# State attention and a hard-swish feed-forward on one NeuronCore: the second softmax's exponentials moved through DRAM, and heads paired four apart

## The chip, the cores and the metric

The kernel runs on one core of a Trainium2 chip. The metric is the device time of one execution in microseconds (us), median of several runs. The program's five engines run side by side, each in the order of its own queue: TensorE (PE; its weight loads are shown as PEld), VectorE (DVE), ScalarE (ACT), GpSimd (POOL) and SyncE (SP), which here issues nearly all DMAs.

## The reference

Two parts. An attention between tokens and a small state, for 8 batches and 8 heads, with 512 tokens, 32 states and 64 features a head:

```python
scores = scale * x @ state^T;   a  = softmax(scores)     # over 32 states
xread  = a @ state
scores2 = scale * state @ x^T;  a2 = softmax(scores2)    # over 512 tokens
sread  = a2 @ x
y = concatenate([xread, sread], tokens)                  # 544 rows a batch, 8 x 64 features
```

and a feed-forward over the 8 x 544 rows: `h = y @ w_in` (512 to 2048), `g = h * clip(h + 3, 0, 6) / 6`, `out = g @ w_out` (2048 to 512). `x` and `state` come as float32, the two weights as float64.

## The kernel before

**Tiling and stages.** The hidden width of 2048 is taken in two sweeps of 1024. In each sweep the 8 batches' 512 tokens are units of eight steps (one step is 128 hidden columns); between the sweeps stand two units for the 8 x 32 state rows. `xread @ w_in` is never made by way of `xread`: the kernel multiplies `state` into `w_in` first (`wprime`, W'), and then the weights `a` with W'. Products run in three passes of float32 parts (`hi*hi + hi*lo + lo*hi`), with ACT making each `hi` and DVE each `lo` (`split`). In the second sweep seven half-size products stand for eight (`seconds`, line 1164).

**The attention of batch b** (1 to 7) runs beside the first sweep of batch b-1. `load_turned` (line 611) brings `x[b]` in blocks of 32 x 32 by DMA and DVE turns the blocks (line 725). `scores_by_columns` (859) multiplies it with the state on PE. `tokens_by_columns` makes `a`, `states` (899) the exponentials of the second softmax, with 128 rows that are states of four heads, two such groups. For `sread` the exponentials must be turned so that tokens lie on partitions: DVE turns their 32 x 32 blocks (line 971), and `weights_moved` (951) then puts the blocks in place by 16 DMAs from SBUF to SBUF a batch (line 979), each 32 partitions and 256 pieces of 128 bytes. `tokens_read` (988) multiplies them with `x` on PE (line 1007); for b > 0 it rides in the same PE entry as the next batch's scores, so that entry waits for the moves and for the next batch's turned `x` alike.

**Pairing.** A partition row of 128 features is a pair of heads (2q, 2q+1), for q = 0 to 3, in `w_in`, `x` and `state` alike. `load_turned` therefore takes 16 transfers a batch, one for each head and half of its features: 64 KB, 512 pieces of 128 bytes. `w_in` comes in 13 transfers (`weight`, line 484), each over all 128 partitions.

**The order.** All work is entered in a `Plan` (line 141) with an engine, a cost, what it reads and writes and, for DMAs, a size and a number of pieces. `Plan.order` is a list scheduler at build time: of what could start within 0.3 us it takes the entry with the least rank, and the ranks are the 2701 numbers in `RANKS` (line 24). The result is a fixed order for each of the five queues. A DMA stands in SP's queue with its wait: what is behind it is not issued before it. `first_of[n]` is the PE entry of step n; up to the first of them, at 19.4 us, filler transposes (line 1642) are put on PE where the plan has a gap; no filler comes after.

Of the kernel before, what the change touches and what calls it, by code (L numbers as in the profile page):

```python
# [10 lines left out]
F32 = mybir.dt.float32  # L11
# [273 lines left out]
def tile_state_attention_then_hardswish_ffn(  # L285
# [38 lines left out]
    kept = ctx.enter_context(tc.tile_pool(name="kept", bufs=1, space=bass.MemoryType.DRAM))  # L324

    x_v = x.rearrange("b h (j p) d -> b j p h d", p=P)
    st_v = state.rearrange("b (q u) n d -> b q n u d", u=NG)

    ident = cpool.tile([P, P], F32, name="ident")
    make_identity(nc, ident)  # L330
# [1342 lines left out]
```

## Time and profile before

| | |
|---|---|
| median of 3 runs | 647.98 us (646.3 to 648.6) |
| the profiled execution | 644.92 us, of which 642.6 us are the span from the first to the last instruction |
| PE busy | 632.0 us, 98% of the span; 4386 matmuls |
| DVE, ACT, POOL busy | 520.6, 346.1, 18.3 us |
| granted TensorE clock | 1.00 throughout |
| DMA | 82.52 MB in 162326 packets, 129760 of them under 512 bytes |

PE counts as busy from the start of a matmul to its modelled end, and matmuls overlap: one of 512 columns lasts 0.39 us, but the next begins 0.23 us after it. So the loss on PE is read from the start of one to the start of the next, not from the busy share. Issuing a DMA is not counted as busy time of SP; how long an issue took is read from the timeline, the chain of waits and the view of a line.

### The profile page before, as it was taken

Reading aid. Unit: us, or ns where it says so; the run is one execution under the profiler, and the core shown is the slowest. Engines: PE = TensorE matmul, PEld = TensorE weight load, DVE = VectorE, ACT = ScalarE, POOL = GpSimd, SP = SyncE. Lnnn points to the kernel's source line nnn. Section 1 sums busy time; section 2 is a strip of 40 time slices with the busy share of each in tenths; the row PEclk is TensorE's granted clock in tenths of the full one; section 3 lists DMA queues with packets and bytes.
Section 4 is the critical chain, followed back from the end, with each engine's and each line's share of the span. In section 5 each row is a group of like instructions: output and inputs, shape, how many; then the busy total and the mean of one; then the engine's idle time right before and its main releaser. Section 6 shows DMA issues by size and latency. Waiting matters only on the chain.

```text
span 642.6 us, 11571 instructions
## 1 busy us (share of the span) xinstructions
PE 632.0 (98%) x4386; PEld 525.5 (82%) x4386; DVE 520.6 (81%) x946; ACT 346.1 (54%) x611; POOL 18.3 (3%) x22
## 2 busy tenths in 40 slices
PE   8999999999999999999999999999999999999997
PEld 6466867877677768778898887999999999999996
DVE  5998788988878859787388837999999888979873
ACT  5866444555456543545365747666464655464441
POOL 0000000000000000000000000000001000001100
PEclk9999999999999999999999999999999999999999
DMA  8986695957749648343303876153524442522433
GB/s 301 267 194 145 163 174 100 239 96 194 149 85 249 165 114 158 91 75 94 70 14 119 275 253 210 50 132 67 132 34 99 99 91 33 116 58 34 65 67 66
DMA packets 162326, 82.52 MB, mean 128 GB/s; under 512 B 129760, under 2 KB 147040, under 8 KB 162144
## 3 DMA queue, kind: packets, MB, share of 16 engines
q1 hardware_dynamic: 158304, 73.80, 44.9%
q0 software_dynamic: 3824, 7.87, 8.4%
q8 instruction: 34, 0.56, 0.4%
q14 instruction: 20, 0.16, 0.1%
q10 hardware_dynamic: 144, 0.13, 0.1%
HBM read 47.17 MB, written 30.93 MB: 122 GB/s over the span
## 4 chain that ended last, share of the span: by engine, by line
PE 80%; DMA 6%; DVE 6%; SPq 5%; ACT 2%; issue 2%; DVEq 0%; ACTq 0%
PE ps_h L1052 27%; PE acc L1164 23%; PE acc L1052 23%; DMA raw<-in_x_dram 2%; SPq L979 2%; SPq L622 2%; PE ps_s L635 1%; DMA raw<-in_moe_w_out_dram 1%; PE acc L1337 1%; PE ps_s L1473 1%; DMA early<-in_moe_w_in_dram 1%; DMA raw<-in_moe_w_in_dram 1%; PE acc L1473 1%; DVE g L1308 1%; PE ps_h L1007 1%
## 5 line engine op out<-in xcount | busy, mean ns | idle before, releaser
L1052 PE MATMUL acc<-w_out_hi,g_hi 128*128 128x512 f32 x296 | 118.5, 400 | 0.1
L1052 PE MATMUL acc<-w_out_hi,g_lo 128*128 128x512 f32 x296 | 115.5, 390 | 0.6 <-DVE g_lo L408 0.6
L1052 PE MATMUL acc<-w_out_lo,g_hi 128*128 128x512 f32 x296 | 115.5, 390 | 0.0
L1164 PE MATMUL acc<-w_out_hi,tmp 128*128 128x256 f32 x360 | 88.9, 283 | 0.0
L1052 PE MATMUL ps_h<-aT_hi,wp_hi 128*128 128x512 f32 (+1 forms) x228 | 84.1, 369 | 1.6 <-DVE wp_lo L408 0.8
L1305 ACT ACTIVATE g<-ps_h,three 128x512 f32<-128x512 f32 (+1 forms) x80 | 51.2, 647 | 62.1 <-PE ps_h L1052 54.9
L1052 PE MATMUL ps_h<-aT_lo,wp_hi 128*128 128x512 f32 (+1 forms) x228 | 82.4, 361 | 0.0
L1052 PE MATMUL ps_h<-aT_hi,wp_lo 128*128 128x512 f32 (+1 forms) x228 | 82.1, 360 | 0.0
L1289 ACT ACTIVATE G<-ps_h,three 128x512 f32<-128x512 f32 x64 | 43.9, 690 | 55.0 <-PE ps_h L1052 45.8
L1052 PEld LDWEIGHTS acc<-w_out_hi,g_hi 128*128 128x128 f32 x296 | 55.6, 188 | 19.4 <-issue 6.1
L1308 DVE SCALAR_TENSOR_TENSOR g<-g,ps_h 128x512 f32<-128x512 f32 (+1 forms) x80 | 49.8, 629 | 26.2 <-ACT g L1305 25.9
L1164 PE MATMUL acc<-w_out_hi,g_lo 128*128 128x256 f32 x240 | 67.9, 283 | 0.0
L1164 PE MATMUL acc<-w_out_lo,g_hi 128*128 128x256 f32 x240 | 67.9, 283 | 0.0
L1164 PE MATMUL acc<-w_out_hi,g_hi 128*128 128x256 f32 x240 | 67.8, 282 | 0.0
L1164 PEld LDWEIGHTS acc<-w_out_hi,tmp 128*128 128x128 f32 x360 | 66.7, 192 | 0.3
L1052 PEld LDWEIGHTS acc<-w_out_hi,g_lo 128*128 128x128 f32 x296 | 55.6, 188 | 13.5 <-DVE g_lo L408 1.4
L1052 PEld LDWEIGHTS acc<-w_out_lo,g_hi 128*128 128x128 f32 x296 | 55.6, 188 | 10.7 <-issue 0.3
L407 ACT CAST g_hi<-g 128x512 fp32r<-128x512 f32 (+1 forms) x74 | 42.3, 585 | 36.2 <-DVE g L1308 18.7
L408 DVE TENSOR_TENSOR g_lo<-g,g_hi 128x512 fp32r<-128x512 f32 (+1 forms) x74 | 46.3, 639 | 11.5 <-ACT g_hi L407 8.2
L1291 DVE SCALAR_TENSOR_TENSOR G<-G,ps_h 128x512 f32<-128x512 f32 x64 | 43.4, 683 | 12.6 <-ACT G L1289 12.1
L407 ACT CAST g_hi<-G 128x512 fp32r<-128x512 f32 (+1 forms) x64 | 38.0, 605 | 28.6 <-PE acc L1164 20.1
L1052 PEld LDWEIGHTS ps_h<-aT_hi,wp_hi 128*128 128x128 f32 x228 | 43.1, 189 | 11.8 <-DVE G L1291 1.7
(167 smaller groups left out, 1236.6 us busy)
## 6 DMA issues: line engine op xcount, KB each, us to landing
out_dram<-ot SPq DMA_DIRECT2D x8, 1024.0 KB, 4.6
W<-G SPq DMA_DIRECT2D x16, 512.0 KB, 4.0
out_dram<-ot POOLq DMA_DIRECT2D x15, 512.0 KB, 5.7
raw<-in_x_dram SPq DMA_DIRECT2D x112, 64.0 KB, 3.3
xb<-in_x_dram SPq DMA_DIRECT2D x28, 256.0 KB, 4.3
raw<-in_moe_w_out_dram SPq DMA_DIRECT2D x11, 511.8 KB, 5.8
wp_lo<-W SPq DMA_DIRECT2D x40, 128.0 KB, 3.0
raw<-in_moe_w_in_dram SPq DMA_DIRECT2D x8, 511.0 KB, 4.4
```

The costliest lines, as they stand in the source:

```text
L407: first = S_(cost, rank, lambda: nc.scalar.copy(hi(), src()), reads, [writes[0]], after)
L408: V(cost, rank, lambda: nc.vector.tensor_tensor(lo(), src(), hi().bitcast(F32), op=ALU.subtract), [*reads, writes[0]], [writes[1]])
L622: nc.sync.dma_start(t[rows, i].rearrange("t (a c) -> t a c", c=NS), x[b, 4 * g + 2 * i + u, :, k * NS : (k + 1) * NS].rearrange("(a t) c - ...
L635: nc.tensor.matmul(out[u][cols, :], made["stT", b][rows, cols], moving(q)[rows], start=True, stop=True,)
L979: nc.sync.dma_start(dst[:, :, q], src[:, :, c])
L1052: nc.tensor.matmul(ps, l, r, start=start and k == 0, stop=stop and k == n - 1)
L1164: nc.tensor.matmul(out, left(a, l), right(b, r), start=p == 0 and z == 0 and y == 0, stop=p == FPS // 2 - 1 and y == 2, skip_group_check=True)
L1289: S_(0.68, n - 1.5, lambda: nc.scalar.activation(g(), by_pass(), AF.Relu, bias=three, scale=-1.0 if turned_sign(FPS + i) else 1.0), [ps], ...
L1291: V(0.63, n - 1.5, lambda: nc.vector.scalar_tensor_tensor(g(), g(), 6.0, by_pass(), op0=ALU.min, op1=ALU.mult), [ps], [g_key])
L1305: in_turn["g", n] = S_(cost + 0.05, rank, lambda: nc.scalar.activation(g(), bank(ps)[:, :width], AF.Relu, bias=three, scale=-1.0 if turned ...
L1308: V(cost, rank, lambda: nc.vector.scalar_tensor_tensor(g(), g(), 6.0, bank(ps)[:, :width], op0=ALU.min, op1=ALU.mult), [ps], [g_key])
L1473: nc.tensor.matmul(bank(banks[q // 2][u])[:, q % 2 * W : (q % 2 + 1) * W], st[l]()[rows, q], wp(r)[rows, q], start=y == 0, stop=y == 2, sk ...
```

## The change

Nothing is added to or taken from PE's, DVE's or ACT's work; the transfers, the pairing of heads and the ranks change.

- `weights_moved`: four transfers write the turned blocks of a batch to a DRAM tile (`there`, 32 x 32 x 128 floats; each 32 partitions, 1024 pieces of 128 bytes), and one (`back`) reads the 512 KB tile into SBUF in place, 1024 pieces of 512 bytes. `back` waits for the four. It was 16 transfers within SBUF.
- Heads are paired four apart: (q, q+4). The two heads of one slot in `load_turned` are then neighbours, so one transfer brings two: 8 a batch of 128 KB and 1024 pieces, for 16. `state`'s views, batch 0's `x` and the index in `tokens_read` follow the pairing.
- A row of `w_in` on the partitions is then no even stride, so each of its 13 loads becomes two of 64 partitions (`load(u)`).
- The plan's cost of `wprime` is entered lower (0.18 + 0.85 a chunk for 0.26 + 0.95), which touches the order alone.
- `RANKS` is new: 2581 numbers. The 120 entries less are 56 for `x`, 77 for the moves, and 13 more for `w_in`. The order of all queues may differ from before.

```diff
@@ RANKS: 2701 numbers before, 2581 after @@
...
@@ -324,7 +319,7 @@
     kept = ctx.enter_context(tc.tile_pool(name="kept", bufs=1, space=bass.MemoryType.DRAM))
 
     x_v = x.rearrange("b h (j p) d -> b j p h d", p=P)
-    st_v = state.rearrange("b (q u) n d -> b q n u d", u=NG)
+    st_v = state.rearrange("b (u q) n d -> b q n u d", u=NG)
 
     ident = cpool.tile([P, P], F32, name="ident")
     make_identity(nc, ident)
@@ -340,7 +335,7 @@
     nc.gpsimd.memset(apart, 0.0)
 
 
-    w_in_v = w_in.bitcast(U16).rearrange("(q p) e -> p q e", p=P)
+    w_in_v = w_in.bitcast(U16).rearrange("(u q d) e -> u d q e", u=NG, q=NQ)
     w_out_v = w_out.bitcast(U16).rearrange("(f p) e -> p f e", p=P)
 
     BANKS = {f"acc{j}": 1 for j in range(J)} | {"ps_h": 2, "ps_s": 2}
@@ -473,15 +468,16 @@
             t = t.rearrange("p i e -> p (i e)").rearrange("p (q f) -> p q f", q=NQ)
             return t if i is None else t[:, :, i * P : (i + 1) * P]
 
-        def load():
+        def load(u=0):
             t = pieces().bitcast(U16)
             flat = t.rearrange("p i e k -> p i (e k)")
             if kind == "in":
                 flat = flat.rearrange("p i e -> p (i e)").rearrange("p (q e) -> p q e", q=NQ)
-                src = w_in_v[:, :, 4 * k * P + 1 : 4 * (k + n) * P]
-            else:
-                src = w_out_v[:, k : k + n, 1:]
-            nc.sync.dma_start(flat[:, :, : flat.shape[2] - 1], src)
+            flat = flat[:, :, : flat.shape[2] - 1]
+            if kind == "out":
+                nc.sync.dma_start(flat, w_out_v[:, k : k + n, 1:])
+                return
+            nc.sync.dma_start(flat[u * D : (u + 1) * D], w_in_v[u, :, :, 4 * k * P + 1 : 4 * (k + n) * P])
 
         def top_of(i):
             t = tops[:, plan.home["top", (kind, k + i)]]
@@ -503,14 +499,17 @@
                 d, low, 13, top_of(i).bitcast(U32), op0=ALU.logical_shift_right, op1=ALU.bitwise_or
             )
 
-        Q(load_rank, 524.288 * n, load, writes=[key], pieces=128 * n if kind == "out" else 512,
-          late=2.0 if k >= FPS else 0.5)
+        late = 2.0 if k >= FPS else 0.5
+        keys = [(*key, "u", u) for u in range(NG)] if kind == "in" else [key]
+        for u in range(len(keys)):
+            Q(load_rank, 524.288 * n / len(keys), lambda u=u: load(u), writes=[keys[u]],
+              pieces=128 * n if kind == "out" else 256, late=late)
         lo = key + ("lo",)
         wide = 0.08 + 0.54 * n
         for i in range(n):
             top = ("top", (kind, k + i))
-            S_(0.62, rank, lambda i=i: upper(i), [key], [top])
-            V(0.62, rank, lambda i=i: join(i), [key, top],
+            S_(0.62, rank, lambda i=i: upper(i), keys, [top])
+            V(0.62, rank, lambda i=i: join(i), [*keys, top],
               w_in_keys(k + i, k + i + 1) if kind == "in" else [(*lo, i)])
         if kind == "in":
             return
@@ -602,8 +601,8 @@
         load_state(0, rank)
         for q in range(NQ):
             hs = slice(q * NG, (q + 1) * NG)
-            def load(hs=hs):
-                nc.sync.dma_start(raw()[:, hs], x[0, hs].rearrange("h (p j) d -> p h j d", j=J))
+            def load(hs=hs, q=q):
+                nc.sync.dma_start(raw()[:, hs], x[0, q::NQ].rearrange("h (p j) d -> p h j d", j=J))
             Q(rank + 0.1 * q, 262.144, load, writes=[(*raw_key, q)], pieces=256, late=0.5)
             V(0.37, rank, lambda hs=hs: nc.vector.tensor_copy(x_tile(0)[:, hs], raw()[:, hs]),
               [(*raw_key, q)], [(*key, "q", q)])
@@ -613,19 +612,16 @@
 
         for g in range(NG):
             key = ("raw", ("x", b, g))
-            for i in range(2):
-                for u in range(2):
-                    for k in range(D // NS):
-                        def load(g=g, i=i, u=u, k=k, key=key):
-                            t = get(key, lambda: stage.tile([P, 2, S], F32, name="raw"))
-                            rows = slice((u * D // NS + k) * NS, (u * D // NS + k + 1) * NS)
-                            nc.sync.dma_start(
-                                t[rows, i].rearrange("t (a c) -> t a c", c=NS),
-                                x[b, 4 * g + 2 * i + u, :, k * NS : (k + 1) * NS].rearrange(
-                                    "(a t) c -> t a c", t=NS
-                                ),
-                            )
-                        Q(rank, 140.0, load, writes=[(*key, i, u, k)], after=after, pieces=512, cost=0.54)
+            for u in range(NG):
+                for k in range(D // NS):
+                    def load(g=g, u=u, k=k, key=key):
+                        t = get(key, lambda: stage.tile([P, 2, S], F32, name="raw"))
+                        rows = slice((u * D // NS + k) * NS, (u * D // NS + k + 1) * NS)
+                        heads = slice(NQ * u + 2 * g, NQ * u + 2 * g + 2)
+                        nc.sync.dma_start(
+                            t[rows].rearrange("t i (a c) -> t (i a) c", c=NS),
+                            x[b, heads, :, k * NS : (k + 1) * NS].rearrange("h (a t) c -> t (h a) c", t=NS))
+                    Q(rank, 280.0, load, writes=[(*key, u, k)], after=after, pieces=1024, cost=0.54)
 
     def all_heads(b, out, moving):
 
@@ -672,7 +668,7 @@
             for c, _, _, n, fs, bs in work:
                 all_heads(b, [bank(key)[:, :n] for key in bs], lambda q: w_in_of(units[k][0] * CPS + c)[:, q, fs])
 
-        at = T(0.26 + sum(0.95 * w[3] / CH for w in work), rank, run,
+        at = T(0.18 + sum(0.85 * w[3] / CH for w in work), rank, run,
                [("stT", b)] + [key for c, f0, f1, *_ in work for key in w_in_keys(
                    units[k][0] * FPS + c * FPC + f0, units[k][0] * FPS + c * FPC + f1)],
                [key for w in work for key in w[5]], after)
@@ -711,7 +707,7 @@
                     for k in range(NG):
                         nc.tensor.matmul(
                             out[..., k], made["st_raw", b][:, k],
-                            ident.rearrange("p (q u m) -> p q u m", q=NQ, u=NG)[:, :, u], start=True, stop=True)
+                            ident.rearrange("p (u q m) -> p q u m", q=NQ, u=NG)[:, :, u], start=True, stop=True)
             turned_first[0] = T(0.65, rank, turn_first, [("st_raw", b)], [st], after)
 
         def put_state():
@@ -724,7 +720,7 @@
                 key = ("raw", ("x", b, q // 2))
                 V(0.7, rank, lambda q=q, key=key: nc.vector.transpose(
                     xT(b, q), made[key][:, q % 2]),
-                    [(*key, q % 2, u, k) for u in range(2) for k in range(D // NS)], [xT_key(b, q)], after)
+                    [(*key, u, k) for u in range(2) for k in range(D // NS)], [xT_key(b, q)], after)
                 continue
             ps = (banks[q] if banks else "ps_s", ("T", b, q))
 
@@ -971,13 +967,19 @@
             V(0.62, rank, lambda g=g: nc.vector.transpose(
                 made_of(blocks_key)[:, g], tmp(("tmp", ("e2", b, g)))),
                 [("tmp", ("e2", b, g))], [(*blocks_key, g)])
-        for c in range(P // NS):
-            for q in range(NQ):
-                def move(c=c, q=q):
-                    src = made_of(blocks_key)[quarter(q)].rearrange("p g (j c n) -> p (g j) c n", j=J, n=NS)
-                    dst = made_of(e2T_key(b, 0))[quarter(c)].rearrange("p g (j q n) -> p (g j) q n", j=J, n=NS)
-                    nc.sync.dma_start(dst[:, :, q], src[:, :, c])
-                Q(rank, 60.0, move, [(*blocks_key, g) for g in range(NG)], [e2T_key(b, 0, c, q)], pieces=256, cost=0.66, late=0.5)
+        there = lambda: get(("kept", (b, "e2")), lambda: kept.tile([NG * S // NS, NS, P], F32, name=f"e{b}"))
+        for q in range(NQ):
+            def move(q=q):
+                nc.sync.dma_start(
+                    there()[:, :, quarter(q)].rearrange("m r n -> r m n"),
+                    made_of(blocks_key)[quarter(q)].rearrange("p g (m n) -> p (g m) n", n=NS))
+            Q(rank, 140.0, move, [(*blocks_key, g) for g in range(NG)], [("kept", (b, "e2"), q)], pieces=1024, cost=0.6)
+
+        def back():
+            nc.sync.dma_start(
+                made_of(e2T_key(b, 0)).rearrange("p g (j m) -> p (g j) m", m=P),
+                there().rearrange("(y c) r m -> (c r) y m", c=P // NS))
+        Q(rank, 524.0, back, [("kept", (b, "e2"), q) for q in range(NQ)], [e2T_key(b, 0)], pieces=1024, cost=0.5)
 
     def put(c, ps, cols):
         V(0.28, URGENT, lambda: nc.vector.tensor_copy(
@@ -991,8 +993,7 @@
         x_parts = [(*read_key(b), "q", q) for q in range(NQ)] if b == 0 else [
             (*read_key(b), j) for j in range(J)]
         t_key = ([e2T_key(b, g) for g in range(NG)] if b == 0 else
-                 [e2T_key(b, g, c, q) for g in range(NG if b < TURNED else 1)
-                  for c in range(P // NS) for q in range(NQ)])
+                 [e2T_key(b, 0)])
         pr, sr_key = (tag, ("D", b)), ("tmp", ("sr", b))
         by_group = lambda t: t[:, : NG * D].rearrange("p (u d) -> p u d", u=NG)
 
@@ -1007,7 +1008,7 @@
                         nc.tensor.matmul(
                             bank(pr)[cols, u * D : (u + 1) * D],
                             e2T(b, u)[:, j * P + q * NS : j * P + (q + 1) * NS],
-                            x_tile(b, True)[:, NG * q + u, j, :],
+                            x_tile(b, True)[:, NQ * u + q if b else NG * q + u, j, :],
                             start=(j == 0),
                             stop=(j == J - 1),
                         )
```

## Rows read from the trace of the kernel before

**Rows 1.** The page's first part: engine, busy us, share of the span, instructions.
```profile
PE 632.0 (98%) x4386; PEld 525.5 (82%) x4386; DVE 520.6 (81%) x946; ACT 346.1 (54%) x611; POOL 18.3 (3%) x22
```

**Rows 2.** Stretches: us, busy us (instructions) by engine, granted clock, DMA share, GB/s.
```profile
20.00:240.00 220.00, 216.39 (x1461) 158.10 (x1467) 184.98 (x335) 124.50 (x218) 0.00 (x0) 1.00 0.71 164
...
400.00:639.00 239.00, 239.00 (x1640) 222.32 (x1638) 205.35 (x378) 124.93 (x223) 17.41 (x15) 1.00 0.38 77
639.00:642.60 3.60, 0.06 (x1) 0.00 (x0) 0.76 (x2) 0.00 (x0) 0.00 (x0) 1.00 0.22 73
```

**Rows 3.** What PE waited for: us in total, times, longest us.
```profile
PE ps_s L712 <- DMA st_raw<-in_state_dram: 1.1, 1, 1.1
PE ps_h L1052 <- DVE wp_lo L408: 0.8, 1, 0.8
...
PE ps_h L1007 <- DMA raw<-raw: 0.8, 2, 0.6
PE acc L1052 <- DVE g_lo L408: 0.6, 1, 0.6
...
PE ps_h L1052 <- DVE ot L408: 0.3, 1, 0.3
PE ps_h L1052 <- DVE g L1308: 0.2, 1, 0.2
```

**Rows 4.** Timeline of PE: start us, us, instruction, [idle before, its releaser].
```profile
106.53 0.39 PE L1052 MATMUL ps_h<-aT_lo,wp_hi 128*128 128x512 f32 x1
106.76 0.39 PE L1052 MATMUL ps_h<-aT_hi,wp_lo 128*128 128x512 f32 x1
107.35 0.50 PE L1052 MATMUL ps_h<-aT_hi,wp_hi 128*128 128x512 f32 x1 [0.20 <-DVE g L1308]
...
110.73 0.40 PE L1007 MATMUL ps_h<-xb,raw 128*32 128x64 f32 x4 [0.59 <-DMA raw<-raw]
```

**Rows 5.** The chain that ended last, 95 to 165 us: start us, us, what.
```profile
100.93 0.61 SPq L979
...
109.28 1.96 DMA raw<-raw
...
155.64 3.25 SPq L622
...
160.00 2.47 DMA raw<-in_x_dram
...
163.89 1.20 PE acc L1052 x4
```

**Rows 6.** Lines that issue DMAs: issue ns min/median/max, first and last start us.
```profile
L622 SPq DMA_DIRECT2D raw<-in_x_dram x112: 311/488/3255, 22.0 to 250.7; - x112
...
L979 SPq DMA_DIRECT2D raw<-raw x112: 585/609/1397, 68.4 to 307.4; - x112
...
L593 SPq DMA_DIRECT2D xb<-in_x_dram x28: 384/488/5663, 60.8 to 280.6; - x28
...
L484 SPq DMA_DIRECT2D early<-in_moe_w_in_dram x5: 384/469/796, 3.2 to 23.2; - x5
```

**Rows 7.** DMA issues: count, KB each, median us from issue to landing.
```profile
raw<-in_x_dram SPq DMA_DIRECT2D x112, 64.0 KB, 3.3
...
a<-tmp SPq DMA_DIRECT2D x14, 256.0 KB, 2.7
...
aT_lo<-a SPq DMA_DIRECT2D x7, 512.0 KB, 4.4
```

**Rows 8.** The page's third part: a DMA queue's packets, MB, share of 16 engines.
```profile
q1 hardware_dynamic: 158304, 73.80, 44.9%
```

**Rows 9.** The chain's pieces on DVE in the start.
```profile
11.85 0.63 DVE raw L502
...
15.96 0.60 DVE w_in L502
```

**Rows 10.** Timeline of PE: the first product of a step.
```profile
19.40 3.68 PE L1269 MATMUL ps_h<-w_in,tmp 128*128 128x512 f32 x8
```

221 rows, old and new, of the table RANKS are left out of this document.

## The prediction

> **What bounds the kernel now.** I read the busy shares first: PE 98%, DVE 81% [rows 1]. The stretches then show that PE's share is no mean over unlike stages: from 400 us to the last product PE is busy the whole time, and after 639 us only the last stores are left, 3.6 us [rows 2]. Between 20 and 240 us, the first sweep, PE is busy 216.4 of 220 us, DVE 185.0, and the DMA engines 0.71 of the time [rows 2]. So the change, whose instructions run from 22 to 307 us [rows 6], can win only what PE loses in the first sweep or before it. It doesn't touch PE's own work: the same 4386 matmuls [rows 1].
>
> How much PE loses there is in the list of its waits. Leaving out the start, five entries stand in the first sweep: 0.8 (W' part late from DVE), 0.8 (the moved exponentials, two times), 0.6, 0.3 and 0.2 us, together 2.7 us [rows 3]. A wait costs more than its idle time. Matmuls of 512 columns start 0.23 us apart (106.53, 106.76); over the 0.20 us wait the step is 0.59, so 0.36 is lost, 0.16 more than the wait [rows 4]. Six waits by 0.16 make about 1.0, so the whole loss is some 3.7 us: 1.1 at the moved exponentials, 2.6 at the four others.
>
> Then the chain of waits says what stands behind these. Before the product at 110.7 stand the sixteen issues of line 979 one after another, 0.61 us each with 0.04 between, and then the landing of the last, 1.96 us [rows 4, 5]. Before the late `g_lo` that PE waits for until 163.89 stand issues of line 622, one of which took 3.25 us, and a landing of 2.47 us of `x` for which DVE stood still [rows 5]. Both lead to SP's queue. That is where the change takes work away.
>
> **The change part by part.** *SP's issues.* Removed are 56 transfers of `x` at 0.49 + 0.04 us, 29.7 us, and 112 moves at 0.61 + 0.04, 72.8 us [rows 5, 6]. Added are 28 writes, which the trace doesn't show in this form: between 0.49 (line 593, as many pieces) and 3.26 us (the longest of line 622, when the queue was full) [rows 6]; I take 0.65, that of line 979, the same tile read in pieces of the same size: 18.2 us. Seven reads back at 0.46, the early weight loads' least 0.38 to their median 0.47 [rows 6]: 3.2 us. Thirteen more loads of `w_in` at 0.47 + 0.04: 6.6 us. Net, SP has 74.5 us less to issue in 285 us. A transfer of `x` of 1024 pieces is not dearer to issue than one of 512: line 593 has 1024 and the same median, 488 ns [rows 6]. [...]
>
> *Time from the first move to usable data.* Before: 15 issues at 0.65 and a landing of 1.96, 11.7 us [rows 5]. After: the last of four writes is issued at 1.95 and lands 2.7 later, as the stores of `a` do [rows 7], at 4.6 us; `back` lands 4.4 later, as the 512 KB reads of `a` do [rows 7]: 9.0 us. From above, still without any penalty for DRAM: the queue took 512 pieces of `x` every 0.53 us [rows 6], so 4096 pieces take up to 4.2 us, with 2.0 for the landing and 4.4 for the read 10.6 us. So the exponentials come 1.1 to 2.7 us earlier, and the two waits for them, 1.1 us with their restarts, go. Next late at that PE entry is the next batch's turned `x`, which the same queue brings and which comes earlier too. I take the whole 1.1; bounds 1.1 and minus 1.1, if other reads come to wait.
>
> *A wait is added.* `back` waits in SP's queue for four writes, 2.7 to some 4.3 us after the last issue. Behind it stand transfers of `x` and the weights, for which DVE (line 725) and ACT wait. Against it stand the 7.2 us a batch that SP saves at the moves (16 x 0.65 less 4 x 0.65 less 0.46, and 0.1 for gaps). So what is behind is issued earlier by 2.9 us or more even if nothing useful stands between.
>
> *The four other waits*, 2.6 us, are DVE results that are late. One of them leads to `x` transfers by the chain [rows 5]; for the others DVE's load of 185 in 220 us [rows 2] is as good a reason. I count half, 1.3 us; bounds 2.6, and minus 2.6 where the new order makes as many of its own.
>
> *`w_in` in halves.* Before the first product at 19.40 us [rows 10] three of its loads become six: 3 x 0.51 = 1.5 us more on SP, in front of the loads of `w_out`. The path to the first product runs through batch 0's softmax on DVE, which `w_out`'s late arrival doesn't hold, so I count nothing. If that cover is gone it costs up to 1.5 us. On the other side two joins of weight digits stand among the softmax steps, 0.63 and 0.60 us [rows 9]; if the new ranks put them behind, the start is up to 1.2 us shorter. Batch 0's `x` has as many transfers and pieces as before, and the pairing of its heads costs nothing.
>
> *Bytes.* The reads back are new traffic: 7168 packets of 512 bytes. The mean packet of SP's queue took 0.449 x 642.6 x 16 / 158304 = 29 ns of one engine [rows 8], so 13 us of all sixteen in 285 us, 0.05 on a share of 0.71 [rows 2]. That alone stays hidden.
>
> *The pieces' size.* In this trace pieces of 128 bytes only come out of DRAM (`x`) or stay in SBUF (the moves); none goes into DRAM. [...]
>
> The sum: 1.1 + 1.3 = 2.4 us. On the profiled execution, 644.92 us (642.6 and 2.3 around the span), that gives 642.5. The median of the runs shown is 3.06 us above that execution, so 645.6 us.
>
> **The rivals.**
> *More is won.* All 3.7 us of waits go and the two joins leave the start: 4.9 us, 643.1. For it: the chain leads to SP in both places looked at. Against it: DVE stays at 84% in that stretch.
> *Nothing is won.* The late DVE results are late because DVE is full, the two waits for the exponentials turn into waits for `x`, and the new order has stalls like the old: 648.0, give or take 2. [...]
> *Slower: small writes into DRAM.* If a piece of 128 bytes into DRAM takes twice the time of one of `x`, the four writes take 8.4 us, and the way is 8.4 + 2.0 + 4.4 = 14.8 us, 3.1 later than before. Seven reads wait for it, and PE's order is fixed, so the loss is up to 21.7 us; of the seven only two waited before, so the others had some slack, and I take half, 10.9 us: 658.9. It decides from the point where the 4096 pieces take over 11.7 - 2.0 - 4.4 = 5.3 us, 1.3 times what `x` takes. While `back` stands, `x` of the next batch also stands behind it. [...]
>
> **How the numbers follow.** Forecast 0.48, its own range 643.4 to 647.4 (a gain of 0.6 to 4.6 us: the 1.1 with none or all of the 2.6, and 0.9 for the start either way); more 0.17; nothing 0.17; slower 0.18. For the slower case 1.3 times is not far, but a write to DRAM of 2 KB pieces lands in 2.7 us without a sign of trouble, and what is late there is first covered by slack. About 0.5%, 3.2 us, is what a measurement of this kernel can tell from no change: below 644.7 or above 651.2. Faster by more: 0.16 of the second case and 0.20 of the first, 0.36. Slower by more: 0.15 of the last and 0.01 of the third, 0.16. Within: 0.48. The range, 642.0 to 650.5, leaves out some 0.04 below (all bounds together, start included) and 0.15 above.
>
> **What would show it.** In the profile after: SP's issues of `x` halved in number with a median near 0.5 us; the writes near 0.65 us each; from the first write to the landing of `back` 9 to 10.6 us (over 11.7: the slower case); no PE wait for `raw` at the read of tokens; PE's waits in the first sweep near 1.3 us in place of 2.7; the first product within a us of 19.4; from 400 us on nothing changed but the offset. The prediction is wrong if PE waits at several of the seven reads, if DVE's waits for `x` grow behind a standing `back`, or if the start moves by over 1.5 us.

## The result, and the profile after

The changed kernel takes 653.71 us (median of 4, 653.13 to 654.62), the kernel before 648.19 us beside it (4 runs, 646.3 to 648.6): a ratio of 1.0092, 95% interval 1.0069 to 1.0115. It is slower by 0.9%, above the range of the forecast. The profiled execution took 654.62 us, its span 652.8 us. Against the profiled execution of before, 644.92 us, that is 9.7 us, more than the 5.5 between the medians: that one lies at the fast end of its runs.

PE's work is the same but for 16 more filler transposes. The profile page's first part, and the stretches (us, busy us and instructions by engine, granted clock, DMA share, GB/s):

```profile
PE 635.9 (97%) x4402; PEld 529.4 (81%) x4402; DVE 521.9 (80%) x946; ACT 343.4 (53%) x611; POOL 18.3 (3%) x22
```

```profile
20.00:240.00 220.00, 211.84 (x1481) 155.05 (x1482) 186.33 (x338) 120.44 (x213) 0.00 (x0) 0.98 0.91 183
400.00:639.00 239.00, 238.86 (x1657) 222.31 (x1657) 210.32 (x387) 129.15 (x233) 16.42 (x15) 1.00 0.39 83
```

Against [rows 1, 2]: from 400 us to the last product nothing is different but the offset. In the first sweep the DMA engines are busy 0.91 of the time, not 0.71, for 183 GB/s against 164: 28% more time for 12% more bytes. (The share adds up the times of all packets over 16 engines, so it can pass 1.)

What PE waited for (us in total, times, longest us):

```profile
PE ps_s L631 <- DVE w_in L498: 3.0, 1, 3.0
PE ps_h L1053 <- DVE g L1309: 2.2, 1, 2.2
...
PE ps_h L1008 <- DMA raw<-e: 1.0, 1, 1.0
PE acc L730 <- DVE xb L607: 0.9, 2, 0.6
PE ps_h L1053 <- DVE aT_lo L403: 0.7, 1, 0.7
PE acc L1053 <- DVE g_lo L403: 0.6, 1, 0.6
```

The two longest are new against [rows 3], and both lie in the first 45 us, by PE's timeline:

```profile
22.39 3.60 PE L1270 MATMUL ps_h<-w_in,tmp 128*128 128x512 f32 x8
29.01 0.67 PE L631 MATMUL ps_s<-w_in,stT 64*32 64x256 f32 x16 [3.02 <-DVE w_in L498]
...
43.98 0.77 PE L1053 MATMUL ps_h<-aT_hi,wp_hi 128*128 128x512 f32 x1 [2.24 <-DVE g L1309]
44.55 0.63 PE L1053 MATMUL ps_h<-aT_lo,wp_hi 128*128 128x512 f32 x1
44.98 0.63 PE L1053 MATMUL ps_h<-aT_hi,wp_lo 128*128 128x512 f32 x1
...
47.70 0.39 PE L1053 MATMUL ps_h<-aT_hi,wp_hi 128*128 128x512 f32 x1
47.92 0.39 PE L1053 MATMUL ps_h<-aT_lo,wp_hi 128*128 128x512 f32 x1
```

The first product comes at 22.39 us, not 19.40 [rows 10]. Behind the second wait the matmuls start 0.43 us apart (44.55, 44.98), not 0.22 (47.70, 47.92). The stretches behind both waits show a mean granted clock of 0.57 and 0.52 of full: by the trace's records the clock was 0.50 for 3.4 us from 30.3 us, 1.3 us behind the end of the 3.02 us wait, and for 3.4 us from 44.0, where the 2.24 us wait ended. At half pace that is some 3 us more, an estimate from these two times:

```profile
30.00:34.00 4.00, 4.00 (x6) 1.36 (x7) 2.79 (x6) 3.59 (x8) 0.00 (x0) 0.57 1.02 172
...
44.00:47.50 3.50, 3.50 (x9) 2.78 (x10) 3.50 (x6) 2.75 (x4) 0.00 (x0) 0.52 1.04 315
```

One thing about this column has to be known. The view shows 1.00 also where the trace has no record of the clock, and the records begin only at 4.7 us before and at 6.4 us after. Until then PE ran at its lower pace in both: matmuls of 128 columns started 213 ns apart, behind it 109. So the "1.00 throughout" of the kernel before holds from 4.7 us on.

I laid the two executions over each other by the PE work still to be done, worked out from all matmuls at their steps; what a step is priced at moves these figures by up to 1 us. The changed kernel is 3.0 us behind at its first product, some 11 at 42 us of the time before, then 9.8 at 274 and 8.6 to 8.8 from 438 us to the last product. So all of this loss, and more, arises in the first 45 us, ahead of the first of the moves through DRAM (75.1 us); behind that the change wins some 2 us. The spans differ by 10.2 us: another 1.4 come behind the last product, where the last store of 128 KB landed in 3.2 us and not in 1.8.

The chain of waits up to 50 us says through what (start us, us, what):

```profile
3.24 5.46 DMA early<-in_moe_w_in_dram
...
8.72 13.33 DMA early<-in_moe_w_in_dram
...
33.51 7.51 DMA early<-in_moe_w_in_dram
...
41.12 0.77 ACT tops L493
...
41.92 1.32 DVE w_in L498 x2
43.24 0.61 DVE g L1309
```

Half a load of `w_in`, 511 KB, took 13.33 us to land. The wait for `g` at 43.98 is one for `w_in` too: DVE stood for it and made `g` late. The page's list of DMA issues (KB each, median us to landing) has for the early loads, first before, then after:

```profile
early<-in_moe_w_in_dram SPq DMA_DIRECT2D x3, 1023.0 KB, 8.8
```

```profile
early<-in_moe_w_in_dram SPq DMA_DIRECT2D x6, 511.5 KB, 10.8
```

Half the bytes take longer, though these times hold the wait behind earlier transfers too. The stretches of the start, before and then after, show that it isn't only a queue that stands:

```profile
10.00:15.00 5.00, 5.00 (x62) 3.60 (x59) 4.89 (x10) 4.73 (x10) 0.00 (x0) 1.00 1.04 397
15.00:20.00 5.00, 4.52 (x55) 3.16 (x43) 4.93 (x11) 3.36 (x9) 0.00 (x0) 1.00 1.08 345
20.00:30.00 10.00, 9.24 (x36) 3.33 (x34) 9.23 (x20) 9.25 (x19) 0.00 (x0) 1.00 1.05 282
```

```profile
10.00:15.00 5.00, 4.44 (x64) 3.83 (x63) 3.33 (x6) 3.62 (x9) 0.00 (x0) 1.00 1.04 331
15.00:20.00 5.00, 4.62 (x42) 2.79 (x40) 4.79 (x12) 2.69 (x5) 0.00 (x0) 1.00 1.07 198
20.00:30.00 10.00, 6.79 (x47) 4.04 (x48) 6.13 (x14) 4.98 (x12) 0.00 (x0) 1.00 1.07 240
```

The DMA engines are full in both; between 15 and 20 us, at shares of 1.08 and 1.07, they move 345 GB/s before and 198 after. Worked out from the trace's packets between 15 and 20 us, one of 2046 bytes, which is a piece of a row of `w_in`, takes 97 ns before and 180 after. The early loads are 3 x 1023 + 2 x 511 KB, 4.2 MB; at 345 GB/s they take 12.1 us of full engines, at 198 GB/s 21.2, 9.0 us more. This estimate is most of the 11 by which the kernel is behind at 42 us; the lower clock after the waits adds to it.

### The profile page after: what moved, and what is told of

It reads as the page before. It is cut to its first block, busy times and chain, and to the rows that moved or that the text cites. A ratio compares the mean times of both kernels' runs of the same rounds, so it can differ in the third digit from the quotient of the medians.

```text
span 652.8 us, 11434 instructions
## 1 busy us (share of the span) xinstructions
PE 635.9 (97%) x4402; PEld 529.4 (81%) x4402; DVE 521.9 (80%) x946; ACT 343.4 (53%) x611; POOL 18.3 (3%) x22
## 4 chain that ended last, share of the span: by engine, by line
PE 82%; DMA 9%; DVE 5%; ACT 1%; SPq 1%; issue 1%; DVEq 0%; ACTq 0%
PE ps_h L1053 27%; PE acc L1053 25%; PE acc L1165 23%; DMA early<-in_moe_w_in_dram 4%; DMA raw<-in_moe_w_in_dram 3%; PE ps_s L631 2%; DMA early<-in_moe_w_out_dram 1%; PE ps_s L1474 1%; PE ps_h L1008 1%; PE acc L1474 1%; DMA raw<-e 1%; ACT tops L493 1%; PE ps_h L631 1%; DVE g L1309 1%; DVE tmp L721 1%
```

## The experiments

Theory: a transfer into one half of the partitions moves its bytes at about half the rate, and nothing else of the change loses time. Rivals: the extra issues; some other part of the change (order, pairing, moves); that the halves read rows of DRAM lying close together.

**The halves alone, in the kernel before.**

```diff
-            nc.sync.dma_start(flat[:, :, : flat.shape[2] - 1], src)
...
+            for u in range(2):
+                nc.sync.dma_start(flat[u * D : (u + 1) * D], src[u * D : (u + 1) * D])
```

> The kernel before with one edit: each of the 13 loads of w_in is issued as two transfers of 64 partitions, as in the changed kernel, in the same place of SP's queue; pairing, moves and ranks are those of before. Theory A (a transfer into 64 partitions moves its bytes at little more than half the rate): packets of 2046 bytes take about 180 ns in place of 97, PE waits for weights in the first 60 us, and the time goes up by 6 to 11 us, to 654 to 659. Theory B (the new ranks made the loss, the halves cost only 13 more issues of about 0.5 us): at most 1.5 us more, 648 to 650. Theory C (the clock drop after idle stretches is the first cause): no drop here without late weights, so as B.

Measured: 662.16 us beside 647.08, ratio 1.0211 (1.0167 to 1.0255). Packets of 2046 bytes take 168 ns. The stretch from 15 to 20 us, and two of PE's waits: the longest is in the start again, at 28.7 us, and later ones for DVE's results have grown:

```profile
15.00:20.00 5.00, 4.11 (x49) 2.04 (x48) 4.54 (x11) 3.37 (x8) 0.00 (x0) 1.00 1.06 262
```

```profile
PE acc L1342 <- DVE g L1313: 3.5, 1, 3.5
PE ps_h L1057 <- DVE ot L408: 2.3, 2, 1.4
```

So this one edit costs more than the whole change does, without new order, pairing or moves.

**Two transfers as well, each over all partitions** (two of the four row blocks each): as many issues, no half of the partitions. The edit is shown against the kernel with the halves alone:

```diff
-                nc.sync.dma_start(flat[u * D : (u + 1) * D], src[u * D : (u + 1) * D])
+                nc.sync.dma_start(flat[:, 2 * u : 2 * u + 2], src[:, 2 * u : 2 * u + 2])
```

> The control to the first: as many transfers of the same bytes and the same packets, but each over all 128 partitions with two of the four row blocks of w_in. Theory A: packets of 2046 bytes stay near 100 ns and the time within 1.5 us of before, 647 to 650. If the count of transfers itself were the cause, the time would go up as in the first, 654 to 659. Theory B: 648 to 650 as well.

Measured: 645.93 us, ratio 0.9976 (0.9951 to 1.0001); 95 ns a packet, and the same stretch:

```profile
15.00:20.00 5.00, 4.53 (x52) 2.46 (x51) 4.86 (x12) 3.24 (x7) 0.00 (x0) 1.00 1.07 350
```

The 13 further issues cost nothing that shows.

**Every second partition and row,** shown against the kernel with the halves alone:

```diff
-                nc.sync.dma_start(flat[u * D : (u + 1) * D], src[u * D : (u + 1) * D])
+                nc.sync.dma_start(flat[u::2], src[u::2])
```

> The first experiment (the kernel before, each w_in load in two transfers of 64 partitions) with one difference: one half takes the even partitions and rows, the other the odd ones, so each half lies over the whole height of SBUF. If it matters where the 64 partitions lie (a contiguous half reaches only half of the way into SBUF): packets of 2046 bytes near 100 ns, no late weights, 646 to 650 us. If it is the count of 64 partitions, 4 for each DMA engine, whatever their place: 160 ns or more and 657 to 663 us as in the first.

Measured: 651.20 us beside 648.80, ratio 1.0043 (1.0018 to 1.0068); 97 ns. The rate is back with 64 partitions a transfer. A late start remains: the first product comes 5.6 us later than before, at 24.99 us. Two things stand there. In this execution the records of the clock begin at 21.2 us, and until then PE ran at its lower pace (eleven transposes from 17.91 us took 2.61 us, from 12.43 us before 1.42); in the run with paired `x` below, where `w_in` comes whole, the same goes with a start 5.2 us late. And block 0's halves had landed at 7.82 and 9.62 us, but ACT's first reader of it began at 14.14, behind the landing of block 1's (13.99). PE waited 0.6 us for that here, and 4.1 us in the run below where the partitions alone are interleaved. What ties strided halves of neighbouring blocks together was not tried, and the two causes are not told apart.

**Which side decides: partitions or rows.** Each half takes every second row and writes 64 contiguous partitions; then the reverse.

```diff
+                nc.sync.dma_start(flat[u * D : (u + 1) * D], src[u::2])       # one kernel
+                nc.sync.dma_start(flat[u::2], src[u * D : (u + 1) * D])       # the other
```

> The kernel before, with each w_in load split into two transfers of 64 contiguous partitions, as in the changed kernel, but each half reads every second of the 128 rows of w_in that the load brings. The rows then lie at other partitions than the state's features, so this part of the result differs; all work and all bytes are the same. Theory A (what slows a half is that it writes into one contiguous half of the partitions): slow packets as in the split by contiguous rows, 2046-byte packets of 155 to 185 ns between 15 and 20 us, and a time near 660 us. Theory B (what slows it is that it reads contiguous rows of DRAM, so that reads lie close together): full rate, 2046-byte packets of 85 to 105 ns, and 645 to 652 us.

> The mirror of the run with interleaved rows: each half of a w_in load writes every second partition and reads 64 contiguous rows of w_in. The rows again lie at other partitions than the state's features, so this part of the result differs. Theory A (the contiguous half of the partitions is what is slow): full rate, 2046-byte packets of 85 to 105 ns, 648 to 655 us (the start about 4 us later, as in the split by even and odd partitions, where the first reader of a block began with the next block's landing). Theory B (contiguous rows of DRAM are slow): packets of 155 to 185 ns, 655 to 665 us.

Measured, one run each beside 646.13: 661.5 and 650.21 us. The stretch from 15 to 20 us, contiguous partitions first, every second partition second:

```profile
15.00:20.00 5.00, 5.00 (x41) 3.71 (x48) 3.65 (x8) 3.01 (x6) 0.00 (x0) 1.00 1.04 256
```

```profile
15.00:20.00 5.00, 4.49 (x34) 3.99 (x35) 4.30 (x9) 4.05 (x10) 0.00 (x0) 0.50 1.07 351
```

| kernel | partitions of a transfer | rows of `w_in`, in each row block | mean of the 2046-byte packets, 15 to 20 us (number) |
|---|---|---|---|
| before | 128 | contiguous | 97 ns (787) |
| after | 64 contiguous | contiguous | 180 ns (459) |
| halves alone | 64 contiguous | contiguous | 168 ns (172) |
| rows interleaved | 64 contiguous | every second | 157 ns (328) |
| partitions interleaved | every second | contiguous | 95 ns (769) |
| both interleaved | every second | every second | 97 ns (777) |
| two row blocks each | 128 | contiguous | 95 ns (824) |

Each row is one execution and one stretch of it. The partitions decide: with 64 contiguous ones the packets take 157 to 180 ns, else 95 to 97, whichever rows are read. What moves the time between 157 and 180 is open, and so is why contiguous halves are slow: the runs show the rates alone.

**The changed kernel without the halves:** `w_in` by its old rows in one transfer.

```diff
-            nc.sync.dma_start(flat[u * D : (u + 1) * D], w_in_v[u, :, :, 4 * k * P + 1 : 4 * (k + n) * P])
+            if u == 0:
+                nc.sync.dma_start(flat, w_in_v[:, :, 4 * k * P + 1 : 4 * (k + n) * P])
```

(with `w_in_v` as before)

> The changed kernel with one edit: w_in is loaded by the old rows, in one transfer of 128 partitions in the place of the first half, so the features of w_in no longer belong to the heads of x (that part of the result is another; instructions and bytes are the same). Against the changed kernel it gives the price of the halves; against the new order with whole w_in and old pairs it gives the worth of 8 transfers of x a batch for 16. Theory A: 643.5 to 647. If the 56 fewer transfers of x matter: 1 us or more below the 645.7 of that kernel; if not, within 1 us of it.

Measured: 640.82 us beside 648.80, ratio 0.9871 (0.9814 to 0.9928). PE's waits, but for the 1.6 us for `ident` that the kernel before has too, are 1.6 us in all:

```profile
PE ps_h L1054 <- DVE aT_lo L403: 0.8, 1, 0.8
PE acc L827 <- DVE w_in L819: 0.4, 1, 0.4
PE acc L731 <- DVE xb L608: 0.2, 1, 0.2
PE ps_s L795 <- DVE sread_t L785: 0.2, 1, 0.2
```

So in the changed kernel the halves cost 653.7 less 640.8, 12.9 us (by the two ratios, each against the runs of before beside it, 2.2%, some 14 us), and the rest of the change wins 1.3%.

**The changed order with the old pairing:** whole loads of `w_in`, and each entry of `x` sends two transfers.

```diff
-                        heads = slice(NQ * u + 2 * g, NQ * u + 2 * g + 2)
...
+                        for i in range(2):
+                            nc.sync.dma_start(
+                                t[rows, i].rearrange("t (a c) -> t a c", c=NS),
+                                x[b, 4 * g + 2 * i + u, :, k * NS : (k + 1) * NS].rearrange(
+                                    "(a t) c -> t a c", t=NS))
```

> The changed kernel with its ranks and its moves through DRAM, but heads paired as before: w_in comes in one transfer of 128 partitions in the place of the first half (nothing in the place of the second), and x in 16 transfers a batch, two in the place of each one. Theory A: the packets take near 100 ns again, the first product comes within 1 us of 19.4, the loss of 10 us in the first 45 us goes, and the time is 643 to 647. Theory B (the new ranks lose it, by loading the third block of w_in late): it stays at 652 or more.

Measured: 645.70 us beside 647.08, ratio 0.9966 (0.9935 to 0.9996). The new order isn't what loses time; with the old number of transfers of `x` it wins little.

**The two halves from two queues:** the second half of each load issued by ACT.

```diff
-            nc.sync.dma_start(flat[u * D : (u + 1) * D], w_in_v[u, :, :, 4 * k * P + 1 : 4 * (k + n) * P])
+            (nc.sync, nc.scalar)[u].dma_start(flat[u * D : (u + 1) * D], w_in_v[u, :, :, 4 * k * P + 1 : 4 * (k + n) * P])
```

> The changed kernel with one edit: the second half of each w_in load is issued by ACT's queue, so that both halves can be in flight at once instead of one behind the other. Theory A in the form that each half alone uses only half of the way into SBUF: the halves overlap, packets of 2046 bytes come near 100 to 130 ns, and 645 to 650 us. If 64 partitions are slow whatever else is in flight: 653, or more by the issues on ACT (13 of about 0.5 us). Theory B: 653.

Measured: 654.11 us, ratio 1.0101 (1.005 to 1.0152): no gain, though the packets took 106 ns between 15 and 20 us, where both halves were in flight, and 318 GB/s were moved; between 35 and 40 us, again with both halves sent at one time (31.7 us), they took 179. More than one thing changed here at once: ACT's first half went out ahead of batch 0's `x`, and PE ran at its lower pace until 24.3 us, where the records of the clock begin (matmuls of 128 columns 213 ns apart, behind it 109). So the time decides nothing. Whether two halves in flight at one time move at the full rate is open as well: the window with 318 GB/s says so, the other does not.

**The new pairing over all partitions:** four transfers a load, by row block, each from two runs of 64 rows.

```diff
+            for q in range(2 * u, 2 * u + 2):
+                nc.sync.dma_start(flat[:, q], w_in_v[:, :, q, 4 * k * P + 1 : 4 * (k + n) * P])
```

> The changed kernel with another way to bring w_in for the new pairs: each load as four transfers, one for each slot of the pairing, each over all 128 partitions (two runs of 64 rows of w_in); two in the place of each half. The result is the reference's. Theory A: packets of 2046 bytes near 100 ns, 26 more issues than the changed kernel at about 0.5 us, mostly hidden: 644 to 649, so a version that keeps the pairing and loses nothing. If a transfer from two separate runs of rows is spread over fewer DMA engines, it is slower than the halves: 660 or more.

Measured: 793.27 us, ratio 1.2224 (1.2164 to 1.2283). While the loads run the DMA engines are nearly idle:

```profile
10.00:15.00 5.00, 0.65 (x6) 0.51 (x5) 0.00 (x0) 0.00 (x0) 0.00 (x0) 0.77 0.14 48
15.00:20.00 5.00, 0.00 (x0) 0.00 (x0) 0.69 (x2) 1.20 (x2) 0.00 (x0) 0.50 0.14 47
```

A share of 0.14 is 2.2 of 16 engines, and each transfer has two runs in the source; whether the one sets the other was not tried. A load of this pairing at the full rate in one transfer was not found.

**Moves through DRAM alone,** in the order before: four of the sixteen entries write, the last reads back.

```diff
...
+                    if n < NQ:
+                        nc.sync.dma_start(
+                            there[:, :, quarter(n)].rearrange("m r n -> r m n"),
+                            made_of(blocks_key)[quarter(n)].rearrange("p g (m n) -> p (g m) n", n=NS))
+                    if n == 15:
+                        nc.sync.dma_start(
+                            made_of(e2T_key(b, 0)).rearrange("p g (j m) -> p (g j) m", m=P),
+                            there.rearrange("(y c) r m -> (c r) y m", c=P // NS))
+                    return
```

> The kernel before, its ranks, pairing and loads, and only the moves of the exponentials changed: four writes to DRAM in the place of the first four of the sixteen entries, the read back in the place of the last, nothing in the eleven between. Theory D (the bounce is harmless and what it frees on SP is worth little, since most waits of PE have other causes): within 1.5 us of before, 645.5 to 648.5. Theory of the forecast (the two waits for the exponentials go, and part of the late DVE results): 644 to 646, with no PE wait at the read of tokens. Theory of small writes (slow into DRAM): 655 or more; the changed kernel's trace speaks against it already, its four writes land 4 us after their issue.

Measured: 643.32 us (640.45 to 645.93) beside 648.80, ratio 0.9900 (0.9870 to 0.9931). No wait for the moved exponentials is left. The waits that are, but for the start's 2.8 us for `ident` and `st_raw`:

```profile
PE ps_h L1066 <- DVE wp_lo L408: 1.1, 1, 1.1
PE acc L1351 <- DVE g L1322: 0.8, 1, 0.8
PE acc L1066 <- DVE g_lo L408: 0.7, 1, 0.7
PE acc L635 <- DVE s L820: 0.4, 1, 0.4
PE ps_h L1066 <- DVE g L1322: 0.4, 2, 0.2
PE ps_s L798 <- ACT w_in L739: 0.3, 1, 0.3
```

This version leaves nothing of the work out and is 1.0% faster than the kernel before, and so faster than the changed one.

**Paired transfers of `x` in the order before,** alone and with the moves through DRAM (`w_in` whole in both): the first of two entries sends both heads, the second nothing.

```diff
+                            if (u, k) in sent:
+                                return
+                            sent.add((u, k))
+                            heads = slice(NQ * u + 2 * g, NQ * u + 2 * g + 2)
...
+                                t[rows].rearrange("t i (a c) -> t (i a) c", c=NS),
+                                x[b, heads, :, k * NS : (k + 1) * NS].rearrange("h (a t) c -> t (h a) c", t=NS))
```

> The kernel before with heads paired four apart and one x transfer for two heads, 8 a batch of 128 KB: the first of each two places in SP's queue sends both heads, the second sends nothing. Order, moves within SBUF and ranks are those of before. w_in is loaded whole over 128 partitions by its old rows, which don't fit the new pairing, so that this part of the result differs. The theory that the loss is the half-partition loads alone: 642 to 649 us, ratio 0.990 to 1.002 (56 fewer issues on SP, which the forecast counted at 25 us of SP's time and at next to nothing for the end). The rival, that the doubled x transfers bring part of the loss: over 651 us, ratio over 1.005.

> The run before (order and ranks of before, heads paired four apart, 8 x transfers a batch, w_in whole by its old rows, so that this part of the result differs), and the moves through DRAM beside it: the changed kernel but for the halves of w_in and the new ranks. If the three parts add up, 0.990 (moves alone) times the ratio of the paired x: 638 to 644 us, ratio 0.982 to 0.992; against the changed kernel with whole loads (640.8 us) the difference is what the new ranks are worth. The rival, that the new ranks carry the gain of that kernel: 644 to 648 us, ratio 0.993 to 1.0.

Measured beside 646.13: 646.45 us, ratio 1.0018 (0.9983 to 1.0054), and 643.21 us, ratio 0.9949 (0.9920 to 0.9979). The 56 issues fewer are 29.7 us of SP's time by the forecast (the expectation's 25 is a slip). The paired transfers lose nothing and win nothing that shows in that order, and the gain of the moves stays, 0.5% here and 1.0% above. Both profiled executions have the late start of the clock: its records begin at 21.3 and 20.5 us. The changed kernel with whole loads stood at 0.9871; whether its order wins more than these two parts is at the edge of the intervals (0.9920 and 0.9928).

## Why the prediction was wrong

**The step that failed is "`w_in` in halves".** It priced the 13 further loads as issues, up to 1.5 us, and these are in fact free (two transfers over all partitions: ratio 0.9976). It took for granted that half a transfer takes half the time. The runs showed that a half takes nearly as long as the whole: its packets of 2046 bytes take 180 ns in place of 97, and the halves cost the changed kernel 12.9 us. Part of what it needed stood in the trace of before: the DMA engines are full from 10 to 30 us, 1.04 to 1.08, so that a loss of rate in the loads can become time there. The step's bounds for the start, plus 1.5 and minus 1.2, had no row under them on the rate of a transfer into 64 partitions; such a row is missing before, and the bound should have been wide for that. The cover named for it, that `w_out` comes late without harm, was the wrong one: it was `w_in` itself that came late. One of the signs of being wrong that the prediction names came true: the first product moved by 3.0 us, over the 1.5 named.

**The rival on the slower side named the wrong mechanism.** It had writes of 128 bytes into DRAM. They are no trouble here: the median issue is 632 ns (0.65 us was taken), and most of the writes land 0.7 to 0.9 us behind the one before. SP's queue at a batch after (start us, us, what), where the four landed at 224.78, 226.94, 227.69 and 228.34, and the read back at 232.62:

```profile
222.27 3.52 SPq L973 DMA_DIRECT2D e<-raw  x4
228.42 0.38 SPq L979 DMA_DIRECT2D raw<-e  x1
228.89 8.39 SPq L621 DMA_DIRECT2D raw<-in_x_dram  x8
```

That is 10.35 us from the first write, and the forecast said 9.0 to 10.6; three of the seven batches are in that range and one takes 11.5. The other three take 16.5 to 20.2, over the 11.7 from which that rival decides, but there the new order issues the read back 6.5 to 11.5 us behind the last write. PE waited 1.0 us for one of the seven. No row or run shows the factor two of that rival, which was assumed. In its place stand these: in the trace of after the four writes had landed 5.1 to 9.1 us after the first issue, 6.4 in the median of the seven batches, where the factor gives 10.4; and the moves alone won 1.0%.

**The steps that held.** *The moves* come earlier, but both times were undersized: before it was 12.9 to 13.7 us from first move to last landing in six of seven batches (11.7 taken from the issues), with the moves alone 11.0 to 12.7 in six of seven. The difference, batch by batch 1.0 to 2.2 us where the forecast had 1.1 to 2.7, is right, and both waits went. *SP's issues* of `x` are halved, at 568 ns where 490 were taken. That the 3.26 us issue of line 622 came because the queue was full isn't shown: five transfers were in flight then, and its issues under 0.7 us had 4.3 on average. *The four other waits* were counted at half. With the moves alone 2.1 us of idle time stand in their place (before 2.0); in the changed order with whole loads one of 0.8 is left. In the changed kernel itself PE waits 2.5 us in the first sweep behind the start, 1.0 of it for a read back, not the 1.3 forecast. *From 400 us on* only the offset differs, up to the last stores.

**A slip in the range.** By its own terms, 1.1 with none of the 2.6 and 0.9 for the start, the gain's lower end is 0.2 us and not 0.6. Neither end is near what was measured.

**The gain was undersized as well.** Without the halves the change wins 1.3% where 2.4 us, 0.4%, were expected; the moves alone won 1.0%. In the profiled executions they win less, 2.4 us (642.6 to 640.2) and 1.1 us (to 641.5) of span. The profiled execution of before, 644.92 us, lies at the fast end of its runs, 645.1 to 651.2 beside these two; three of the four kernels with whole loads and without the sixteen moves reach at most 645.9, the fourth (the changed order with the old pairing) 648.5. What makes the runs of before spread so was not found, and so some 5 us of the gain have no place in a trace. One candidate stands in the traces: the time at which PE leaves its lower pace, 4.7 us in the execution of before, and 21.3 and 20.5 in the two with paired `x`, whose starts come some 5 us later. Only one execution of before has a trace, so whether its runs differ in that isn't shown.

## What to carry to other kernels

Count the partitions that a transfer touches as closely as its bytes: where the DMA engines are full, cutting a 128-partition load into two contiguous halves of 64 made its packets take 157 to 180 ns in place of 95 to 97, while cutting it by row blocks cost nothing that shows. A layout that saves transfers in one place can force such halves in another; look where in the kernel the DMA share stands at one. And a part of a change that seems mere form, here the loads made to fit a new pairing, needs its own row for its rate, or else wide bounds.

## What the runs showed of the hardware

- Between 15 and 20 us, with all loads issued by SP, packets of 2046 bytes into 64 contiguous partitions took 157 to 180 ns, into 128 or into every second partition 95 to 97 ns. With the second halves issued by ACT they took 106 ns there and 179 between 35 and 40 us.
- The issue of such a half took 0.61 us (median), that of a whole load 0.47 for the five early ones and 0.41 for the eight later.
- PE's first microseconds run at its lower pace, and how long differs from run to run. In all fourteen traces matmuls of 128 columns start 213 ns apart until the first record of the granted clock and 109 ns behind it where the records say 1.00; the first record comes between 4.6 and 24.3 us. The views show 1.00 ahead of it, where no clock was recorded, so there the pace has to be read from the matmuls. Eleven transposes before (first record at 4.7 us), then the same with paired `x` (21.3 us):

```profile
1.56 2.61 PE L1642 MATMUL ps_h<-ident 128*128 128x128 f32 x11 [1.56 <-POOL ident masks.py:199]
12.43 1.42 PE L1642 MATMUL ps_h<-ident 128*128 128x128 f32 x11
```

```profile
16.92 2.61 PE L1643 MATMUL ps_h<-ident 128*128 128x128 f32 x11
```

- So in the run with paired `x` sixteen matmuls took 3.51 us, which took 1.97 before, and the first product came at 24.55 us, not 19.40 (first row with paired `x`, second before). What decides when the clock first rises was not tried:

```profile
8.71 3.51 PE L799 MATMUL ps_s<-sread_t,w_in 128*128 128x64 f32 x16
```

```profile
7.82 1.97 PE L798 MATMUL ps_s<-sread_t,w_in 128*128 128x64 f32 x16
```
